# Sigmoid attention and a gated feed-forward layer on one core: other places for block sums on VectorE, and one copy on ScalarE

## The chip, the core and the metric

The kernel runs on one core of a Trainium2 chip. A core has five engines that run side by side, each through its own list of instructions and strictly in order: TensorE (PE in the profile; its weight loads are shown apart as PEld), VectorE (DVE), ScalarE (ACT), GpSimd (POOL) and SyncE (SP). Transfers run on 16 DMA engines, fed by queues: here POOL issues the input loads (queue q0), SP issues stores and DMA transposes (queue q1). The metric is the device time of one execution in microseconds (us), as a median of several.

## The reference

Inputs are q, k, v of shape 8 x 12 x 448 x 64 (batch, head, position, head dimension) and three weight matrices. What is computed:

```python
scores = scale * np.matmul(q, k.transpose(0, 1, 3, 2)) - np.log(S)
attn = 1.0 / (1.0 + np.exp(-scores))
attn_out = np.matmul(attn, v)
x = attn_out.transpose(0, 2, 1, 3).reshape(B * S, H * D)      # 3584 x 768
gate = np.maximum(x @ w_gate, 0.0)                            # 3584 x 1536
val = x @ w_val
out = gate * val @ w_out                                      # 3584 x 768
```

The attention is a sigmoid for each score, so it needs no sums over rows.

## The kernel before

**Tiling.** The data is held in fp16. Batches are handled one after another, 0 to 7. In a batch the 12 heads form three groups `g` of four heads, and the 448 keys form seven chunks `c` of 64. A *qk unit* (`qk_unit`, L292) is one chunk of one group: four matmuls into two PSUM banks, and ScalarE's sigmoid of each bank (L187) into a tile `PT`. After all seven chunks of a group, `pv_group` multiplies with v into two banks (28 matmuls), and VectorE scales those into `xT` (L184), the input of the feed-forward layer.

**Feed-forward, plain.** For batches 0 and 1 the layer is computed in the usual way. `gv` (L304) makes 128 of the 1536 hidden units: six matmuls with `wg` into `g_ps`, six with `wv` into `v_ps`, a ReLU of `g_ps` on ScalarE (`gate_sb`, L318) and the product on VectorE, which writes `hT` (L327) and so sets `v_ps` free. These pieces stand in `gv_queue`, and `ffn_mix` takes the next few of them; it also calls *hooks*, pairs of a number and a job, once no more than that number of pieces is left.

**Feed-forward, with block sums.** All else of the layer uses a Strassen-like scheme with seven block products where the usual one has eight. It needs sums and differences of blocks, all made on VectorE (`sub`, L376):
- `weight_sums(i)`, i = 0 to 3: four sums `T[i]` of blocks of `wo`, each 128 x 2304. `T[1]` is made from `T[0]`, and `T[3]` from `T[1]`.
- `token_sums` (L406): sums `S` of blocks of `hT` for one pair of token tiles.
- `gate_sums(f0, f1)` (L477): overwrites the upper half of `wv` by `wg - wv` for hidden tiles f0 and f0 + 1, 128 x 768 at once, six calls in all. This can only be done once the plain `gv` pieces that read those columns of `wv` are through; the plain pieces come in rising order of f.
- `unit_sums` and `batch_sums` for the block products of batches 2 and later.

`down_pair` (L423) makes the output of one pair of token tiles in seven products of six matmuls each, named by their PSUM tiles: b (`u`) = A11 B11; copy of b by `first_copy`; then `beside()`, which runs the jobs handed to it; c (`y12`) = S1 T[0]; b += S2 T[1]; a (`y11`) = A12 B21; b += S3 T[2]; c += S4 B22; b += A22 T[3]. Each accumulation into b must come after the earlier content of b was read out. The read-outs go to `ysb`: scaled copies on VectorE (`scaled`, L416) or ScalarE (`scaled_act`, L421), and multiply-and-add on VectorE (`plus`, L437).

**Transposes.** From batch 2 on, k and q get into the layout of TensorE through `dma_transposes` (L211): VectorE copies k and q of one group into `rel` (L215, two copies), and SP issues a DMA transpose of it into `qkT` (L219), which the qk units read.

**PSUM.** Eight banks are handed out in a ring (`bank`, L76): a tile gets the bank that was handed out eight calls ago (`down_pair` and the block form of the gate and value reorder the ring by `later`). TensorE waits there until the reader of the earlier content is through.

**Order.** The order of instructions is written out by hand: what the Python code emits first stands first in each engine's list. A batch is cut into stages m (`cuts`, L693 to L698). In a stage the qk units are emitted, with a `pv_group` between them, and then a piece of feed-forward work: pieces from `gv_queue` (the number is `mix[m]`), or one item of the list `work` by `next_work` (L675). For group 0 (batches 0 and 1) `work` holds ("y", 0, 0), ("t", 0, 6), ("y", 0, 1) and ("y", 0, 2): three `down_pair`s and one plain tile by `down` (L341).

What matters around the change:
- Batch 2, stage 4 takes one piece of `gv_queue`, stage 5 two, and then the first `down_pair` with the job `dma_transposes(3, 0), dma_transposes(3, 1)`. The four weight sums are hooks in these stages. `wo` is loaded by POOL behind batch 2's v and ahead of batch 3's k, q and v.
- Batch 3 takes one plain piece in each of stages 0, 1 and 2, the plain tile in stage 3, and the second `down_pair` in stage 4. All six `gate_sums` stand behind stage 3.

Of the kernel before, what the change touches and what calls it, by code (L numbers as in the profile page):

```python
# [17 lines left out]
def kernel(  # L18
# [19 lines left out]
    NFC = DF // P  # L38
# [37 lines left out]
    def bank(name, shape=(P, 512), dtype=FP32):  # L76
        pool, tag = free[0]
        free.rotate(-1)
        return pool.tile(list(shape), dtype, tag=tag, name=name)
# [4 lines left out]
    def later(order):  # L84
        keys = [free[i - 8] for i in order]
        for key in keys:
            free.remove(key)
            free.append(key)
# [286 lines left out]
    def sub(o, a, b):  # L375
        nc.vector.tensor_tensor(out=o, in0=a, in1=b, op=AOP.subtract)  # L376
# [5 lines left out]
    def products(jobs):  # L382
        for ps, n, kn, A, W, first in jobs:
            for k_ in range(kn):
                nc.tensor.matmul(  # L385
                    ps[:, 0:n],
                    A[:, k_, :],
                    W[:, k_, :],
                    start=(first and k_ == 0),
                    stop=(k_ == kn - 1),  # L390
                    skip_group_check=True,
                )


    def weight_sums(i):
        T = [late["T"][:, j] for j in range(4)]
        B11, B21 = wo[:, 0:HF, 0:HM], wo[:, HF:NFC, 0:HM]
        B12, B22 = wo[:, 0:HF, HM:DM], wo[:, HF:NFC, HM:DM]
        sub(T[i], *((B12, B11), (B22, T[0]), (B22, B12), (B21, T[1]))[i])

    def token_blocks(g, p):
        h = hT_tiles[g]
        t1, t2 = (slice(t * P, (t + 1) * P) for t in (2 * p, 2 * p + 1))
        return h[:, 0:HF, t1], h[:, HF:NFC, t1], h[:, 0:HF, t2], h[:, HF:NFC, t2]
# [15 lines left out]
    def scaled_act(o, ps):  # L420
        nc.scalar.activation(o, ps[:, 0:HM], AF.Copy, scale=OUT_SCALE)  # L421

    def down_pair(g, p, beside, then, last, first_copy):  # L423
        A11, A12, S3, A22 = token_blocks(g, p)
        S1, S2, S4 = sums.pop(("y", g, p))
        T1, T2, T3, T4 = (late["T"][:, i] for i in range(4))
        B11, B21, B22 = wo[:, 0:HF, 0:HM], wo[:, HF:NFC, 0:HM], wo[:, HF:NFC, HM:DM]
        y1, y2 = (ysbp.tile([P, DM], FP32, tag="ysb", name="ysb") for _ in range(2))
        lo, hi = slice(0, HM), slice(HM, DM)
        b, c, a = bank("u"), bank("y12"), bank("y11")  # L430
        later((7, 6, 5))

        def product(ps, A, W, first=True):
            products([(ps, HM, HF, A, W, first)])

        def plus(o, ps):
            nc.vector.scalar_tensor_tensor(  # L437
                out=o, in0=ps[:, 0:HM], scalar=OUT_SCALE, in1=o, op0=AOP.mult, op1=AOP.add
            )

        product(b, A11, B11)
        first_copy(y1[:, lo], b)
        beside()
        product(c, S1, T1)
        scaled_act(y2[:, hi], c)
        product(b, S2, T2, False)
        scaled_act(y1[:, hi], b)
        product(a, A12, B21)
        plus(y1[:, lo], a)
        if last:  # L450
            store(g, 2 * p, y1, 0, HM, (nc.sync, nc.sync))
        product(b, S3, T3, False)
        plus(y2[:, hi], b)
        if last:
            store(g, 2 * p + 1, y2, HM, DM, (nc.sync, nc.sync))
        product(c, S4, B22, False)
        plus(y1[:, hi], c)
        if last:
            store(g, 2 * p, y1, HM, DM, (nc.sync, nc.scalar))
        else:  # L460
            store(g, 2 * p, y1, 0, DM, (nc.sync, nc.sync))
        then()
        product(b, A22, T4, False)
        if last:
            q3 = slice(0, HM // 2), slice(HM // 2, HM)
            nc.scalar.activation(y2[:, q3[0]], b[:, q3[0]], AF.Copy, scale=OUT_SCALE)
            nc.vector.tensor_scalar(
                out=y2[:, q3[1]], in0=b[:, q3[1]], scalar1=OUT_SCALE, scalar2=None, op0=AOP.mult
            )
            store(g, 2 * p + 1, y2, 0, HM, (nc.sync, nc.scalar))  # L470
        else:
            scaled_act(y2[:, lo], b)
            store(g, 2 * p + 1, y2, 0, DM, (nc.sync, nc.sync))
# [185 lines left out]
    work = deque()  # L659
# [12 lines left out]
            elif kind == "y":  # L672
                token_sums(g, i)

    def next_work(jobs=(), alone=False):  # L675
        kind, g, i = work.popleft()

        def beside():
            for job in jobs:
                job()  # L680

        if kind == "y":
            down_pair(g, i, beside, prepare, not work, scaled_act if alone else scaled)
        elif kind == "w":
            gv_pair(g, i, lambda: (prepare(), beside()), nc.scalar.copy if alone else nc.vector.tensor_copy)
        else:
            beside()
            prepare()
            down(g, i)

    ffn_mix(1, [(1, lambda: both(1, 0))])
    for b in range(1, B):
        if b == 1:  # L693
            cuts, pv_at = (0, 3, 6, 9, 13, 17, 21), {3: (0, 2), 5: (1, 2)}
        elif b == 2:
            cuts, pv_at = (0, 4, 7, 11, 14, 18, 21), {0: (-1, 2), 2: (0, 2), 4: (1, 2)}
        else:
            cuts, pv_at = (0, 4, 8, 12, 16, 21), {0: (-1, 2), 2: (0, 2), 4: (1, 2)}  # L698
        count = len(cuts) - 1
        hooks = {}  # L700
        if b == 1:
            mix = (3, 3, 3, 3, 3, 2)
            hooks = {
                1: [(1, lambda: both(1, 1))],
                3: [(1, lambda: both(1, 2))],
                4: [(3, lambda: dma_transposes(2, 0))],
                5: [(2, late_loads)],
            }
        elif b == 2:
            mix = (2, 2, 1, 1, 1, 2)  # L710
            hooks = {
                2: [(0, prepare)],
                4: [(1, lambda: weight_sums(0)), (0, lambda: weight_sums(1))],
                5: [(1, lambda: weight_sums(2)), (0, lambda: weight_sums(3))],
            }
            open_late()
        elif b == 3:
            mix = (1, 1, 1, 0, 0)
        else:
            mix = (0,) * count  # L720
        for m in range(count):
            jobs = []
            for i, (g, c) in enumerate(order[cuts[m] : cuts[m + 1]]):
                if m in pv_at and i == pv_at[m][1]:
                    if m == 0:
                        pv_finish(b - 1)
                        if b == 2:
                            push_group(0)
                        elif b % 2 == 0:
                            push_group(b // 2 - 1)  # L730
                    else:
                        pv_group(b, pv_at[m][0])
                qk_unit(b, g, c)
            if m == 0 and b > 1:
                jobs.append(lambda: dma_transposes(b, 2))
            if b == 2 and m == count - 1:
                jobs.append(lambda: (dma_transposes(3, 0), dma_transposes(3, 1)))
            elif b == 3 and m == count - 1:
                jobs.append(lambda: (dma_transposes(4, 0), dma_transposes(4, 1)))
            elif 0 <= m - count + 2 and 3 < b < B - 1:  # L740
                jobs.append(lambda: dma_transposes(b + 1, m - count + 2))
            if b == 1:
                if m == 0:
                    load(2, 0, 1, "kq")
                    load(2, 1, 2, "kq")
                    load(2, 2, 3, "kq")
            elif m == 0 and b + 1 < B:
                if b == 3:
                    jobs.append(lambda: hold(3, 2))
                jobs.append(lambda: (load(b + 1, 0, 3, "kq"), load_v(b + 1)))  # L750
            if b % 2 and b > 2:
                if m == count - 1:
                    jobs.append(lambda: (batch_sums_t1(b // 2), batch_sums(b // 2, (0, 1))))
            elif b > 3 and m == 0:
                jobs.append(lambda: batch_sums(b // 2 - 1, (1, HD)))
            if b == 2 and m == count - 1:
                ffn_mix(mix[m], hooks[m])
                next_work(jobs)
            elif mix[m]:
                for job in jobs:  # L760
                    job()
                ffn_mix(mix[m], hooks.get(m, ()))
            else:
                next_work(jobs)
            if b == 3 and m == 3:
                for f in range(0, NFC, 2):
                    gate_sums(f, f + 2)
    pv_finish(B - 1)
    push_group(B // 2 - 1)
# [33 lines left out]
```

## Time and profile before

| | us |
|---|---|
| median of 3 runs | 400.2 (400.01 to 400.21) |
| the profiled execution | 400.3 |
| its span, first to last instruction | 398.5 |
| PE busy | 388.5 (97%) |
| DVE busy | 280.2 (70%) |
| ACT busy | 222.9 (56%) |
| POOL busy | 49.5 (12%) |
| granted TensorE clock, mean | 0.998 |

How to read the profile. Times are counted from the span's start. A line of the timeline gives the start, the length from the first start to the last end, the engine, the line in the kernel, the operation, what it writes and reads, and how many instructions were merged; in brackets stands how long the engine was idle before it and what ended that idle time. Matmuls are pipelined: one group's first matmul starts before the group before it has quite ended, so distances are best taken from start to start. A line of waits names the waiting engine, line and tile, what it waited for, the total, the number of waits and the longest. A line of windows gives the stretch, its length, the busy time of each engine (with the number of instructions), the granted TensorE clock, the mean share of the 16 DMA engines that was busy (it passes 1 where packets overlap) and GB/s. A line of a DMA queue gives packets, MB, and the packets' time as a share of 16 engines. Busy time off the engine that bounds a stage costs nothing there.

The two stretches that the change touches lie at 84 to 101 us (batch 2's last two stages) and at 107 to 130 us (batch 3's stages 1 to 4).

### The profile page before, as it was taken

The numbers are of one execution on the slowest core, as the hardware profiler recorded it, in microseconds if no ns is written. First come the engines' busy times: TensorE is split into PE (matmuls) and PEld (weight loads), VectorE is DVE, ScalarE is ACT, GpSimd is POOL, SyncE is SP. The second block draws the span as 40 slices with busy tenths as digits, with TensorE's granted clock in tenths as the row PEclk, the third lists the DMA queues.
The fourth block names the chain that finished last, engine by engine and source line by source line (L and its number), as shares of the span: only waits on it lengthen the run. The fifth ranks groups of instructions, "written<-read, shape, count | busy, mean of one in ns | idle before, by whom it ended". The sixth has DMA issues, their size and how long they took to land.

```text
span 398.5 us, 8744 instructions
## 1 busy us (share of the span) xinstructions
PE 388.5 (97%) x3488; PEld 217.6 (55%) x3488; DVE 280.2 (70%) x540; ACT 222.9 (56%) x475; POOL 49.5 (12%) x73
## 2 busy tenths in 40 slices
PE   8999999998998999999999999999999999999995
PEld 3678786444455555545555555455455555555563
DVE  2453344357358889999767889999775779987662
ACT  5946778783785465655675455565566233543121
POOL 9643301600030300003000210000000000000000
PEclk9999999999999999999999999999999999999999
DMA  9999994999897894223945696222113320000135
GB/s 149 199 198 205 204 157 81 178 203 178 187 152 152 169 208 79 46 48 43 169 90 133 134 207 109 47 16 55 27 33 88 81 79 2 0 1 2 39 92 147
DMA packets 68953, 43.69 MB, mean 110 GB/s; under 512 B 35888, under 2 KB 65584, under 8 KB 68912
## 3 DMA queue, kind: packets, MB, share of 16 engines
q0 software_dynamic: 30736, 23.33, 39.2%
q1 hardware_dynamic: 37744, 19.34, 23.0%
q8 instruction: 27, 0.44, 0.4%
q10 hardware_dynamic: 432, 0.46, 0.4%
q14 instruction: 14, 0.11, 0.1%
HBM read 47.19 MB, written 11.01 MB: 146 GB/s over the span
## 4 chain that ended last, share of the span: by engine, by line
PE 84%; DMA 10%; POOL 2%; DVE 2%; ACT 1%; issue 1%; ACTq 0%; POOLq 0%; DVEq 0%
PE u L385 32%; PE g L385 15%; PE y L385 9%; PE qk_ps L232 7%; PE pv_ps L250 7%; DMA wg<-in_moe_w_gate_dram 6%; PE g_ps L309 5%; PE v_ps L309 5%; DMA v<-in_v_dram 4%; PE ya L346 3%; PE yb L346 1%; POOL q L110 1%; ACT PT L187 1%; DVE wv L376 1%; POOL k L110 1%
## 5 line engine op out<-in xcount | busy, mean ns | idle before, releaser
L187 ACT ACTIVATE PT<-qk_ps 128x448 f16<-128x448 f32 (+3 forms) x318 | 150.6, 592 | 70.8 <-PE qk_ps L232 70.8
L385 PEld LDWEIGHTS <-S 128*128 128x128 f16 x540 | 52.8, 98 | 44.3 <-issue 0.8
L536 DVE TENSOR_TENSOR gsb<-g,gsb 128x448 f32<-128x448 f32 x72 | 43.0, 625 | 14.6 <-PE g L385 13.8
L232 PE MATMUL qk_ps<-qkT 64*64 64x448 f16 (+2 forms) x756 | 49.7, 336 | 0.8 <-DVE qkT L206 0.5
L421 ACT ACTIVATE ysb<-u 128x384 f32<-128x384 f32 x26 | 13.0, 498 | 52.5 <-PE u L385 52.5
L327 DVE TENSOR_TENSOR hT<-gate_sb,v_ps 128x256 f16<-128x256 f32 (+2 forms) x36 | 16.2, 465 | 33.0 <-ACT gate_sb L318 22.1
L385 PEld LDWEIGHTS <-hT 128*128 128x128 f16 x288 | 27.7, 98 | 21.0 <-issue 3.2
L532 ACT COPY gsb<-u 128x448 f32<-128x448 f32 x48 | 25.7, 564 | 23.9 <-PE u L385 22.9
L250 PE MATMUL pv_ps<-PT,v 64*64 64x448 f16 (+2 forms) x756 | 37.6, 329 | 0.7 <-DMA v<-in_v_dram 0.3
L184 DVE TENSOR_SCALAR xT<-pv_ps 128x448 f16<-128x448 f32 (+2 forms) x53 | 27.9, 566 | 13.8 <-PE pv_ps L250 12.4
L309 PE MATMUL v_ps<-xT,wv 128*128 128x256 f16 (+2 forms) x216 | 33.3, 290 | 0.7 <-DVE hT L327 0.7
L232 PEld LDWEIGHTS <-qkT 64*64 64x64 f16 x756 | 20.2, 105 | 24.9 <-issue 16.1
L309 PE MATMUL g_ps<-xT,wg 128*128 128x256 f16 (+2 forms) x216 | 33.5, 291 | 0.1
L385 PEld LDWEIGHTS <-wv 128*128 128x128 f16 x216 | 21.1, 98 | 19.7
L385 PEld LDWEIGHTS <-wg 128*128 128x128 f16 x216 | 20.3, 98 | 20.6 <-issue 3.0
L250 PEld LDWEIGHTS <-v 64*64 64x64 f16 x756 | 21.8, 107 | 12.4 <-issue 1.3
L385 PE MATMUL u<-T,hT 128*128 128x384 f16 x144 | 27.3, 326 | 0.0
L437 DVE SCALAR_TENSOR_TENSOR ysb<-y,ysb 128x384 f32<-128x384 f32 x24 | 13.4, 557 | 18.8 <-PE y L385 11.3
L110 POOL DMA_DIRECT2D k<-in_k_dram x14 | 10.9, 779 | 113.9 <-DVE rel L215 105.7
L309 PEld LDWEIGHTS <-wg 128*128 128x128 f16 x216 | 18.5, 98 | 11.5 <-issue 5.0
L309 PEld LDWEIGHTS <-wv 128*128 128x128 f16 x216 | 20.1, 98 | 8.3 <-issue 0.9
L385 PE MATMUL u<-xT,wg 128*128 128x448 f16 x108 | 23.5, 353 | 0.1
(69 smaller groups left out, 530.6 us busy)
## 6 DMA issues: line engine op xcount, KB each, us to landing
out_dram<-ysb SPq DMA_DIRECT2D x52, 192.0 KB, 3.0
k<-in_k_dram POOLq DMA_DIRECT2D x5, 672.0 KB, 12.1
q<-in_q_dram POOLq DMA_DIRECT2D x5, 672.0 KB, 14.7
v<-in_v_dram POOLq DMA_DIRECT2D x8, 336.0 KB, 15.5
v<-in_v_dram POOLq DMA_DIRECT2D x16, 168.0 KB, 15.6
k<-in_k_dram POOLq DMA_DIRECT2D x8, 224.0 KB, 10.4
wo<-in_moe_w_out_dram POOLq DMA_DIRECT2D x1, 1536.0 KB, 13.5
q<-in_q_dram POOLq DMA_DIRECT2D x6, 224.0 KB, 11.3
```

What stands on the lines that cost most here:

```text
L110: nc.gpsimd.dma_start(t16[:, xs, cs], rows_of(src, b)[:, xs, cs])
L184: nc.vector.tensor_scalar(out=xT, in0=src, scalar1=XSCALE, scalar2=None, op0=AOP.mult)
L187: nc.scalar.activation(PT_ap, ps_ap, AF.Sigmoid, bias=sig_bias, scale=qk_scale)
L232: nc.tensor.matmul(out_of(hh)[o : o + 64, :], qkT[rows, c, cols], qkT[rows, NCH + c0 : NCH + c1, cols], start=True, stop=True, tile_positi ...
L250: nc.tensor.matmul(ps[hh][64 * r : 64 * r + 64, 0:qn], v16[rows, 2 * g + hh, c * D : (c + 1) * D], pieces[c][rows, hh, :], start=(c == 0), ...
L309: nc.tensor.matmul(ps[-1][:, 0:qn], wt[:, dc, f * P : (f + 1) * P], xT_tiles[b][:, dc, q0 : q0 + qn], start=(dc == 0), stop=(dc == NDC - 1),)
L327: nc.vector.tensor_tensor(out=hT_tiles[g][:, f, o : o + qn], in0=gate_sb[:, 0:qn], in1=ps[1][:, 0:qn], op=AOP.mult,)
L346: nc.tensor.matmul(ps[:, 0 : m1 - m0], hT_tiles[g][:, f, t * P : (t + 1) * P], wo[:, f, m0:m1], start=(f == 0), stop=(f == NFC - 1),)
L385: nc.tensor.matmul(ps[:, 0:n], A[:, k_, :], W[:, k_, :], start=(first and k_ == 0), stop=(k_ == kn - 1), skip_group_check=True,)
L437: nc.vector.scalar_tensor_tensor(out=o, in0=ps[:, 0:HM], scalar=OUT_SCALE, in1=o, op0=AOP.mult, op1=AOP.add)
L532: by(gs[u][i][:], ps[u][:, 0:S])
L536: nc.vector.tensor_tensor(out=gs[u][i][:], in0=ps[u][:, 0:S], in1=gs[u][i][:], op=AOP.add)
```

## The change

Three things move, and no computation changes.

1. The hooks with the four weight sums. In batch 2's stage 4, sums 0 and 1 stood before and behind its one plain piece; now sum 0 stands behind it. In stage 5, sums 2 and 3 stood between its two pieces and behind them; now sums 1 and 2 stand there. Sum 3 becomes a further job of the first `down_pair`, behind the four `rel` copies of the two transposes.
2. In this first `down_pair` the copy of the first product is made by ScalarE instead of VectorE.
3. Of the six `gate_sums` calls of batch 3, the four for hidden tiles 0 to 7 now stand behind stage 1, and two stay behind stage 3.

On VectorE, the list between batch 2's stage 4 and the first `down_pair`'s last accumulations was: sum 0, hT, sum 1, hT, sum 2, hT, sum 3, first copy, four rel copies, three accumulations. It becomes: hT, sum 0, hT, sum 1, hT, sum 2, four rel copies, sum 3, three accumulations. On ScalarE one copy is added. The lists of TensorE, POOL and SP hold the same instructions in the same order.

```diff
-    def next_work(jobs=(), alone=False):
+    def next_work(jobs=(), alone=False, first_act=False):
...
-            down_pair(g, i, beside, prepare, not work, scaled_act if alone else scaled)
+            down_pair(g, i, beside, prepare, not work, scaled_act if alone or first_act else scaled)
...
-                4: [(1, lambda: weight_sums(0)), (0, lambda: weight_sums(1))],
-                5: [(1, lambda: weight_sums(2)), (0, lambda: weight_sums(3))],
+                4: [(0, lambda: weight_sums(0))],
+                5: [(1, lambda: weight_sums(1)), (0, lambda: weight_sums(2))],
...
-                next_work(jobs)
+                next_work(jobs + [lambda: weight_sums(3)], first_act=True)
...
-            if b == 3 and m == 3:
-                for f in range(0, NFC, 2):
+            if b == 3 and m in (1, 3):
+                for f in range(*((0, 8, 2), (8, NFC, 2))[m // 2]):
                     gate_sums(f, f + 2)
```

## The prediction

> **What bounds the kernel now.** I read the page's shares and chain, then who waited for whom with PE as the one that waits, then the timeline around those waits, then the DMA queues there.
>
> ```profile
> PE 388.5 (97%) x3488; PEld 217.6 (55%) x3488; DVE 280.2 (70%) x540; ACT 222.9 (56%) x475; POOL 49.5 (12%) x73
> PE 84%; DMA 10%; POOL 2%; DVE 2%; ACT 1%; issue 1%; ACTq 0%; POOLq 0%; DVEq 0%
> ```
>
> TensorE is busy for 97% of the span. The change touches no matmul, so it can gain only what PE waits for, and can lose only by making PE wait. The waits of PE:
>
> ```profile
> PE u L385 <- DVE xT L184: 1.2, 1, 1.2
> PE v_ps L309 <- DVE hT L327: 0.7, 1, 0.7
> PE u L385 <- DVE ysb L416: 0.6, 1, 0.6
> ```
>
> Three single waits, 2.5 us of idle, all for DVE. Two lie together (batch 2's end):
>
> ```profile
> 87.65 0.76 PE L232 MATMUL qk_ps<-qkT 64*64 64x448 f16 x12
> 88.34 1.31 PE L309 MATMUL g_ps<-xT,wg 128*128 128x448 f16 x6
> 88.38 1.36 DVE L376 TENSOR_TENSOR T<-wo 128x2304 f16<-128x2304 f16 x1 [2.22 <-DMA wo<-in_moe_w_out_dram]
> 89.65 0.61 DVE L327 TENSOR_TENSOR hT<-gate_sb,v_ps 128x448 f16<-128x448 f32 x1
> ...
> 90.32 1.30 PE L309 MATMUL v_ps<-xT,wv 128*128 128x448 f16 x6 [0.67 <-DVE hT L327]
> ...
> 94.53 1.35 DVE L376 TENSOR_TENSOR T<-wo,T 128x2304 f16<-128x2304 f16 x1
> ...
> 95.80 0.55 DVE L416 TENSOR_SCALAR ysb<-u 128x384 f32<-128x384 f32 x1
> 96.27 0.38 DVE L215 COPY rel<-k 128x896 f16<-128x896 f16 x1
> 96.40 1.14 PE L385 MATMUL u<-T,S 128*128 128x384 f16 x6 [0.57 <-DVE ysb L416]
> ```
>
> The first weight sum stands on DVE in front of a hidden-layer product and waits 2.22 us for `wo`; the product behind it frees the PSUM bank that v_ps wants. Later the fourth sum holds up DVE's copy of the first product. The third wait:
>
> ```profile
> 119.85 1.49 PE L250 MATMUL pv_ps<-PT,v 64*64 64x448 f16 x28
> 119.90 2.89 DVE L376 TENSOR_TENSOR wv<-wg,wv 128x768 f16<-128x768 f16 x6
> ...
> 122.71 1.15 DVE L184 TENSOR_SCALAR xT<-pv_ps 128x448 f16<-128x448 f32 x2
> 123.38 1.14 PE L385 MATMUL u<-wo,hT 128*128 128x384 f16 x6 [1.16 <-DVE xT L184]
> ```
>
> Six sums on `wv` stand ahead of the xT scaling; u takes pv's bank.
>
> **Change 1: the weight sums and the ScalarE copy.** With the hidden product ahead of the first sum, hT runs at about 87.8 (v_ps ends at 87.72; the usual lag is 0.10). The g group starts every 1.14 us or so, so v_ps starts at 89.48, not 90.32: **0.83**. The first sum still starts at 88.38, set by `wo`. DVE then has hT at 91.37 (behind ScalarE's gate at 90.70 + 0.60), the second sum at 91.9, hT at 93.2, the third at 93.74, the four rel copies from 95.01 (start to start, a sum takes 1.27, a copy 0.30, an hT 0.54), and the fourth sum at 96.21 to 97.56. PE: u at 92.89, then every 0.975: y 93.87, u 94.85, y 95.82, u 96.80, y 97.77, u 98.75. The last needs the fourth sum: 1.2 us to spare. The third product needs ScalarE's copy: u ends 94.03, the copy takes 0.49 (row of L421), free at 94.6, 0.2 to spare; ScalarE has nothing else then (it idles 2.54 us before its copy at 95.87). That takes away the second wait, 96.40 - 95.67 = **0.73**. The DVE accumulation into `y2`, which the last u needs, is behind the fourth sum and one other: 98.04 to 98.6, before 98.75. The last u moves from 100.30 to 98.75: 1.55 earlier.
>
> But what is late next? The qk of batch 3 behind this pair (PE 101.37 = 100.30 + 1.07, the same 1.07 as at 130.29 and 212.30, so nothing holds it up now) needs the DMA transpose of rel, issued on SP at 97.02, to land 4.1 us after (101.12), 0.25 ahead of its use. The rel copies are only 1.26 earlier, so SP issues at 95.76; q's load, which copy two reads, lands at 95.0 (73.7 + 21.3), just in time. At 4.1 us it would land at 99.86 and qk start near 100.0: a gain of 1.37. However, q0 is then still bringing in batch 3's v (landing 98.4 = 75.9 + 22.5):
>
> ```profile
> 97.00:97.50 0.50, 0.50 (x5) 0.29 (x3) 0.50 (x2) 0.00 (x0) 0.00 (x0) 1.00 0.17 23
> 98.25:98.50 0.25, 0.25 (x3) 0.14 (x2) 0.00 (x0) 0.00 (x0) 0.00 (x0) 1.00 1.00 201
> ...
> q0 software_dynamic: 27, 0.02, 17.2%
> ...
> q0 software_dynamic: 166, 0.15, 90.3%
> q1 hardware_dynamic: 170, 0.04, 32.9%
> ...
> q1 hardware_dynamic: 837, 0.21, 113.8%
> ```
>
> The first two lines are windows (last columns: DMA share, GB/s). From 96.8 to 98.1 the share is 0.17 against 1.26 with all 16 engines at work, so two engines lag with v packets (27 of them from 97 to 98); the transpose's own packets start at 98.2, 1.2 after its issue. From 140 to 141 a load and a transpose run together at one packet each (166 and 170); alone, q1 moves 837 in a microsecond (19 ns an engine). Moved up, the transpose starts at 96.95 and on two engines shares with about 16 v packets each, 69 ns apiece (231 per us over 16): 96.95 + 1.1 + 2.14 (448 KB at 837 packets per 0.21 MB, some 112 packets an engine) + 0.1 for alternating = 100.3, where it was 98.2 + 2.14 = 100.34. So it lands at about 101.0, hardly earlier than now, qk starts at 101.1 or 101.2, and PE idles some 1.3 us. I take **0.2** of the 1.55. Bounds: 1.55 if it lands within 3.9 (the shortest, at 164.1); -0.2 if it takes 5.7, the longest with a quiet q0 (217.4). I stay at 0.2 since the two engines' work is the same in either order.
>
> The Trainium skill, "DMA: Bandwidth & Descriptors", section "Queues, rings and completion order", says that each DMA engine alternates between the queue rows that have work, a packet of several descriptors at a time. It agrees with the 166 and 170 above and speaks against this move: by it the part is worth about 0.2, by the 4.1 us row alone 1.4.
>
> **Change 2: four of the six `wv` sums go to batch 3's second stage.** Two remain ahead of the xT scaling: 119.90 + 2 x 0.47 = 120.85, before pv is done. xT then starts 1.53 after pv's start as at 101.77/103.30: 121.38, freeing the bank at 122.0. PE also has three qk units to finish:
>
> ```profile
> 212.70 1.49 PE L250 MATMUL pv_ps<-PT,v 64*64 64x448 f16 x28
> 214.03 1.04 PE L232 MATMUL qk_ps<-qkT 64*64 64x448 f16 x12
> 215.00 0.28 PEld L385 LDWEIGHTS <-hT 128*128 128x128 f16 x3 [0.20 <-issue]
> ```
>
> Here the same sequence, without sums, has u 2.30 after pv's start. So u starts at 122.15, not 123.38: **1.23**. The bounds are 1.5 (12 qk matmuls in 0.69, as at 87.65) and 1.0 (a scaling 0.2 later). What follows u (first copy, rel copies, X sums, transposes, accumulations) hangs on u and moves with it; ScalarE's sigmoids now end 0.2 after y's product, which delays a copy nobody needs for four products.
>
> The four sums land behind hT at 110.50: 111.04 to 112.91. The xT pair behind them moves from 111.46 to 112.91 and frees its banks at 113.5 and 114.1; the ring of eight hands those to the first qk unit at 114.28. Cost nothing, margin 0.2; beyond it every delay is PE's, up to 0.5 if each sum stretches by 0.15. The next hT (114.46) waits for ScalarE's gate anyway. POOL issues batch 4's loads at 109.74 to 113.4 beside them; its issues took 0.87, 0.83, 0.75 and 1.26 also at 185.0 under a DVE 92 to 100% busy, so they stay. SP's and POOL's order is the same as before; the second and third transposes go out up to 1.4 earlier, and none is needed before 107.
>
> **Sum.** 0.2 + 1.23 = 1.4 us, in a PE-bound rest that only shifts. The profiled execution took 400.3 (span 398.5 and 1.8 around it), 0.1 above the median; from 400.2 I get **398.8**.
>
> **Rivals.**
> - *The transpose is not held up.* For it: 3.9 to 4.1 us in most rows. Against: the two lagging engines. Gain 1.37 + 1.23 = 2.6: 397.6. Chance 0.14.
> - *A transpose completes late.* At 62.7 and 217.4 with a quiet q0 it took 5.5 and 5.7, nothing else differing. If batch 3's first does so atop the sharing, or batch 4's first (0.4 to spare), 1.2 to 1.5 goes: 400.1. Chance 0.11.
> - *The sums in the second stage hold up xT.* Margin 0.2; 0.3 lost: 399.1. Chance 0.10.
> - *Slower: the transpose shares at full load.* If v's load ran on and all engines shared, it would take 10.6 to 12.4 us as at 226.5 and 135.0; issued at 95.76 it lands from 106.4, qk loses 5.1, sum 5.1 - 1.2: 404.1. It decides from a landing past 103.2. Against: q0 falls to 0.17 at 96.8, whatever the change. Chance 0.05.
>
> **How the numbers follow.** 398.8 has 0.60, its own range 398.4 to 399.2. The low end 397.4 takes in the free transpose with its 1.55 bound; the high end 399.9 reaches into the late completion. A measurement tells 0.2% (0.8 us) from nothing, so faster means below 399.4: 0.58 of the main case, all of the free transpose, 0.09 of the xT case: 0.81. Same: 0.02 + 0.01 and 0.09 of the late completion: 0.12. Slower: 0.07.
>
> **What would show it.** Right: neither v_ps near 89.5 nor the third product near 94.8 waits for DVE; last u at 98.7; PE's one new wait is qk for the transpose, 1 to 1.5 us, ending near 101.1; the transpose issued at 95.8 lands 5.2 after; u at 122 or so without a wait. Wrong: a landing 4.1 after the issue, a wait of qk for xT at 114, or a later last u.

## The result, and the profile after

The changed kernel takes 398.21 us (median of six runs, 397.81 to 399.14) against 400.11 for the kernel before: a ratio of 0.9953, 95% interval 0.9941 to 0.9964. It is faster by 1.9 us (1.4 to 2.4), where 1.4 was forecast. In two later comparisons the ratio was 0.9959 (0.9946 to 0.9972) and 0.9949 (0.9936 to 0.9963).

The execution that was profiled is the slowest of the six (399.14, span 397.3). It lost 1.0 us before the change is reached: the gate group of batch 2's stage 4 starts at 86.30 where it started at 85.28, and TensorE had waited for batch 1's v at 47 to 49 us. So positions are compared as distances from one start to another. Two stretches serve throughout:
- *stretch 1*, from the gate group of batch 2's stage 4 to the first qk unit of batch 3: 15.06 us (86.30 to 101.36) after 16.09 (85.28 to 101.37) before;
- *stretch 2*, from the first qk unit of batch 3's stage 4 to the second pair's first product: 2.70 (119.44 to 122.14) after 3.93 (119.45 to 123.38).

Together 2.26 us, and what follows only shifts: from that first product to the end of the span it is 275.2 now and 275.1 before.

Who waited for whom, TensorE as the one that waits, changed kernel:

```profile
PE pv_ps L250 <- DMA v<-in_v_dram: 0.8, 2, 0.5
PE qk_ps L232 <- DVE qkT L206: 0.5, 1, 0.5
PE qk_ps L232 <- DMA qkT<-rel: 0.4, 1, 0.4
```

The three waits for VectorE that the prediction showed are gone, and there is one new one: qk for the DMA transpose. The timeline of the changed kernel, batch 2's end and then batch 3's stages 1 to 4:

```profile
89.37 1.31 PE L309 MATMUL g_ps<-xT,wg 128*128 128x448 f16 x6
89.39 1.35 DVE L376 TENSOR_TENSOR T<-wo 128x2304 f16<-128x2304 f16 x1
...
90.52 1.30 PE L309 MATMUL v_ps<-xT,wv 128*128 128x448 f16 x6
...
96.00 0.39 DVE L215 COPY rel<-k 128x896 f16<-128x896 f16 x1
...
96.75 4.87 SPq L219 DMA_TRANSPOSE qkT<-rel  x2
...
97.21 1.35 DVE L376 TENSOR_TENSOR T<-wo,T 128x2304 f16<-128x2304 f16 x1
...
99.77 1.14 PE L385 MATMUL u<-T,hT 128*128 128x384 f16 x6
...
101.36 0.57 PE L232 MATMUL qk_ps<-qkT 64*64 64x448 f16 x8 [0.45 <-DMA qkT<-rel]
...
111.03 1.96 DVE L376 TENSOR_TENSOR wv<-wg,wv 128x768 f16<-128x768 f16 x4
...
112.91 1.15 DVE L184 TENSOR_SCALAR xT<-pv_ps 128x448 f16<-128x448 f32 x2
...
114.27 1.23 PE L232 MATMUL qk_ps<-qkT 64*64 64x448 f16 x16
...
121.37 1.16 DVE L184 TENSOR_SCALAR xT<-pv_ps 128x448 f16<-128x448 f32 x2 [0.47 <-PE pv_ps L250]
...
122.14 1.15 PE L385 MATMUL u<-wo,hT 128*128 128x384 f16 x6
```

What to see: v_ps now starts 1.15 behind its gate group, without a wait. The pair's last product stands 13.47 behind the first gate group (86.30 to 99.77), as worked out (98.75 - 85.28); the fourth sum, at 97.21, is done in time for it. Then qk comes 1.59 later instead of 1.07: the transpose was issued at 96.75 and landed 4.6 after. At 114.27 the delayed xT scalings cost nothing, and at 122.14 the second pair starts at the place that was forecast (122.15).

### The profile page after: what moved, and what is told of

Read it like the earlier page. It is cut to its first block, busy times and chain, and to the rows that moved or that the text cites. A ratio compares the mean times of both kernels' runs of the same rounds, so it can differ in the third digit from the quotient of the medians.

```text
span 397.3 us, 8744 instructions
## 1 busy us (share of the span) xinstructions
PE 388.5 (98%) x3488; PEld 217.5 (55%) x3488; DVE 279.6 (70%) x539; ACT 223.2 (56%) x476; POOL 49.5 (12%) x73
## 4 chain that ended last, share of the span: by engine, by line
PE 84%; DMA 11%; POOL 2%; ACT 1%; issue 0%; DVE 0%; ACTq 0%; POOLq 0%; DVEq 0%
PE u L385 32%; PE g L385 15%; PE y L385 8%; PE qk_ps L232 7%; PE pv_ps L250 7%; PE g_ps L309 5%; PE v_ps L309 5%; DMA wg<-in_moe_w_gate_dram 4%; DMA v<-in_v_dram 3%; PE ya L346 3%; DMA q<-in_q_dram 2%; PE yb L346 1%; DMA qkT<-rel 1%; ACT PT L187 1%; POOL k L110 1%; POOL q L110 1%
```

## The experiments

Two readings of the new wait were held against each other. *Shared engines*: the transpose is late because the last packets of batch 3's v still occupy DMA engines. *Own time*: a transpose takes 4.1 to 4.6 us after its issue whatever runs beside it, and the prediction saw sharing where there was none. Stretch 1 and the landing tell them apart; the times tell whether a stretch reaches the end.

### The changed kernel again, and each half alone

The first run is the changed kernel as it is.

> The changed kernel once more, as the measure for the three others. Both theories: about 1.9 us less than the kernel before (398.2 against 400.1). From the start of the gate group of batch 2's stage 4 to the first qk of batch 3: 15.1 us (16.09 before, 15.06 in the first profile of the changed kernel). From that first qk unit of batch 3's stage 4 to the first product of the second pair: 2.70 us (3.93 before).

Measured: 398.36 us, ratio 0.9959 (0.9946 to 0.9972), so 1.64 us; stretch 1 15.10, stretch 2 2.70. Then only the `wv` sums:

```diff
-            if b == 3 and m == 3:
-                for f in range(0, NFC, 2):
+            if b == 3 and m in (1, 3):
+                for f in range(*((0, 8, 2), (8, NFC, 2))[m // 2]):
```

> Only the four wv sums are moved. Both theories: 1.23 us less than before, so 398.9. The stretch to batch 3's first qk stays at 16.1 us, the one to the second pair's first product is 2.70 us.

Measured: 398.84 us, ratio 0.9969 (0.9958 to 0.9979), so 1.24 us with 0.84 to 1.68 as the interval; stretch 2 is 2.70. Stretch 1 was expected to stay at 16.1 and was 15.73. Its first wait was smaller in this execution; timeline:

```profile
87.82 1.36 DVE L376 TENSOR_TENSOR T<-wo 128x2304 f16<-128x2304 f16 x1 [1.85 <-DMA wo<-in_moe_w_out_dram]
...
88.16 1.31 PE L309 MATMUL g_ps<-xT,wg 128*128 128x448 f16 x6
...
89.10 0.61 DVE L327 TENSOR_TENSOR hT<-gate_sb,v_ps 128x448 f16<-128x448 f32 x1
...
89.77 1.29 PE L309 MATMUL v_ps<-xT,wv 128*128 128x448 f16 x6 [0.30 <-DVE hT L327]
```

VectorE waited 1.85 us for `wo` instead of 2.22, and TensorE 0.30 instead of 0.67, with the same code in this stretch. The wait that the other half of the change removes is as long as the load of `wo` happens to be late against TensorE, and that differed between these two executions.

The other half alone, the weight sums and the ScalarE copy:

```diff
-            if b == 3 and m in (1, 3):
-                for f in range(*((0, 8, 2), (8, NFC, 2))[m // 2]):
+            if b == 3 and m == 3:
+                for f in range(0, NFC, 2):
```

(against the changed kernel)

> Only the weight sums and the ScalarE copy. By the working of the prediction 0.2 us less than before (399.9), the stretch to batch 3's first qk 15.9. By the profile of the changed kernel 1.0 less (399.1), the stretch 15.1. The second stretch stays at 3.93.

Measured: 399.49 us, ratio 0.9982 (0.9973 to 0.9991), so 0.72 us with 0.36 to 1.08 as the interval; stretch 1 15.01, stretch 2 3.92. The prediction's 0.2 is outside. The halves give 1.24 + 0.72 = 1.96 together; the whole gave 1.64 in this same comparison, with 1.1 to 2.2 as the interval, and 1.9 in the first. They add up within the noise.

### Take the load away from the transpose, and add to it

```diff
-                jobs.append(lambda: (load(b + 1, 0, 3, "kq"), load_v(b + 1)))
+                jobs.append(lambda: (load(b + 1, 0, 3, "kq"), b > 2 and load_v(b + 1)))
...
-                jobs.append(lambda: (dma_transposes(3, 0), dma_transposes(3, 1)))
+                jobs.append(lambda: (dma_transposes(3, 0), dma_transposes(3, 1), hold(3, 0), load_v(3)))
```

> The changed kernel, with batch 3's v loaded only after the first transpose of batch 3 has landed, so that no load runs beside that transpose. Theory of the shared engines: the transpose lands 4.0 to 4.1 us after its issue, qk waits 0.1 or not at all, the stretch is 14.6 to 14.7 and the time 0.4 below the changed kernel's. Theory that the landing takes its own time, whatever q0 carries: 4.6 after the issue again, stretch 15.1, time as the changed kernel's.

Measured: the transpose landed 4.1 after its issue, qk did not wait, and stretch 1 was 14.56. The floor is 14.54, the 16.09 of before less the 1.55 that the last product gains. So the load beside the transpose sets the delay, and *own time* is out. Whether the two share the engines or something else on their way, this run cannot tell. But the time was 399.93, ratio 0.9992: slower than the changed kernel. TensorE's timeline of this run says where it went:

```profile
109.44 0.35 PE L250 MATMUL pv_ps<-PT,v 64*64 64x448 f16 x2
110.25 0.37 PE L250 MATMUL pv_ps<-PT,v 64*64 64x448 f16 x1 [0.46 <-DMA v<-in_v_dram]
111.39 1.51 PE L250 MATMUL pv_ps<-PT,v 64*64 64x448 f16 x25 [0.77 <-DMA v<-in_v_dram]
```

The first value product of batch 3 now waits for v, with some 1.8 us from start to start beyond its usual course (109.44 to 112.56 and not 1.36). That was the run's own price, which its expectation had left out.

The opposite: more load beside the transpose.

```diff
-                jobs.append(lambda: (load(b + 1, 0, 3, "kq"), load_v(b + 1)))
+                jobs.append(lambda: (load(b + 1, 0, 3, "kq"), load_v(b + 1), b == 2 and nc.gpsimd.dma_start(
+                    late["X"][:, 0:2].rearrange("p a k s -> p (a k) s"), rows_of(v, 3)
+                )))
```

> The changed kernel with batch 3's v read once more into a scratch tile right behind the load of v, so that q0 is busy on all engines some 3.4 us longer. Shared engines: the transpose, issued at the same place, gets one packet for one of the load's, lands 7 to 8 us after its issue instead of 4.6, and the stretch grows to about 17.5 to 18.5. Own time: 4.6 and 15.1.

Measured (one run): landing 7.8 after the issue, stretch 1 18.32 (85.55 to 103.87). That is within what was expected of shared engines and far from the own time. The time was 404.27, some 6 us above the changed kernel's, and the wait explains only 3.3 of it; the rest is in the section on the hardware.

### A version that keeps the transpose free

Since only a third of v is needed early, the load can be cut: the third for group 0 where it was, the rest behind the first transpose's landing.

```diff
-                jobs.append(lambda: (load(b + 1, 0, 3, "kq"), load_v(b + 1)))
+                jobs.append(lambda: (load(b + 1, 0, 3, "kq"), load_v(b + 1, 0, 2 if b == 2 else NPAIR)))
...
-                jobs.append(lambda: (dma_transposes(3, 0), dma_transposes(3, 1)))
+                jobs.append(lambda: (dma_transposes(3, 0), dma_transposes(3, 1), hold(3, 0), load_v(3, 2)))
```

(`load_v(b, x0, x1)` loads head pairs x0 to x1.)

> The changed kernel, with batch 3's v loaded in two steps: its first third, which the first value product of batch 3 needs, where it was, and the other two thirds once the first transpose of batch 3 has landed. Shared engines: the first third is in about 2.2 us sooner than all of v was, so most of the sharing goes; the transpose lands 4.1 to 4.3 after its issue, the stretch from the gate group of batch 2's stage 4 to batch 3's first qk is 14.6 to 14.8 instead of 15.06 to 15.10, no value product waits for v, and the time is 0.3 to 0.5 below the changed kernel's (397.9). Own time: 4.6 and 15.1 again, 398.3.

Measured: landing 4.1 after the issue, stretch 1 14.57, no value product of batch 3 waits; 398.0 us, ratio 0.9942 (0.9926 to 0.9958). Run once more on one chip with the changed kernel:

> The changed kernel, beside the next two on one chip: stretch 15.1, 0.4 to 0.5% below the kernel before.

> The kernel with batch 3's v in two steps again, now beside the changed kernel: stretch 14.57 as in its first profile, 0.5 us below the changed kernel if a shorter stretch reaches the end; the same time if it is given back later.

Measured: 398.19 us (0.9949, 0.9936 to 0.9963) for the changed kernel with stretch 1 14.94, and 397.82 (0.9943, 0.9930 to 0.9955) for this one with 14.66. In every profile its stretch is the shorter one, by 0.3 to 0.5, and its median is 0.4 lower; but the intervals overlap, so the time does not prove the gain over the changed kernel. Against the kernel before it is clear.

The windows of the first transpose show the three cases side by side. The stretch, its length, busy time by engine, and at the end the granted clock, the DMA share and GB/s. Before:

```profile
98.50:99.00 0.50, 0.50 (x6) 0.29 (x3) 0.45 (x1) 0.00 (x0) 0.00 (x0) 1.00 1.12 215
99.00:99.50 0.50, 0.50 (x5) 0.30 (x4) 0.11 (x1) 0.00 (x0) 0.00 (x0) 1.00 1.16 214
```

Changed (its transpose's packets start at about 97.9, v's last leave at about 98.7):

```profile
98.50:99.00 0.50, 0.50 (x5) 0.31 (x4) 0.50 (x2) 0.00 (x0) 0.00 (x0) 1.00 1.01 60
99.00:99.50 0.50, 0.50 (x5) 0.30 (x4) 0.46 (x2) 0.00 (x0) 0.00 (x0) 1.00 0.88 114
...
100.00:100.50 0.50, 0.50 (x5) 0.31 (x4) 0.46 (x1) 0.00 (x0) 0.00 (x0) 1.00 1.28 286
```

With v cut in two:

```profile
97.50:98.00 0.50, 0.50 (x5) 0.30 (x4) 0.50 (x2) 0.00 (x0) 0.00 (x0) 1.00 1.12 216
98.00:98.50 0.50, 0.50 (x5) 0.31 (x4) 0.46 (x2) 0.00 (x0) 0.00 (x0) 1.00 1.16 212
```

In these windows the transpose alone moves 212 to 217 GB/s. In the changed kernel the rate falls to 60 GB/s around the end of v, and afterwards it reaches 286. The packets of the changed kernel, by half microseconds from 98.0 to 100.5 (q1 carries the transpose, q0 the load of v; a line of q1 alone is a half microsecond without v):

```profile
q1 hardware_dynamic: 368, 0.09, 155.1%
q0 software_dynamic: 16, 0.01, 16.8%
...
q1 hardware_dynamic: 96, 0.02, 93.4%
q0 software_dynamic: 8, 0.01, 7.2%
...
q1 hardware_dynamic: 223, 0.06, 87.8%
...
q1 hardware_dynamic: 462, 0.12, 128.3%
...
q1 hardware_dynamic: 559, 0.14, 127.8%
```

Alone, before the change, q1 moves 420 and 417 in the half microseconds from 98.5 to 99.5. So the transpose first runs near its rate beside v's last packets, then drops to 96. That is not just two engines' part: at the usual rate the other 14 would have moved some 370. Over the first three half microseconds it falls some 570 packets short, 0.7 us of its work; over the next two it gains some 185, or 0.2 us. The other six profiles with the same load there fall to between 28 and 120 GB/s in their lowest half microsecond. Why the end of a load holds up all of the transpose is not shown. The landing loses 0.3 to 0.5 (4.4 to 4.6 against 4.1), not the 1.1 of the prediction.

### Which of the moved sums matter

First the ScalarE copy undone:

```diff
-                next_work(jobs + [lambda: weight_sums(3)], first_act=True)
+                next_work(jobs + [lambda: weight_sums(3)])
```

> The changed kernel with the first product's copy back on VectorE. The third product of the first pair waits for the copy, which stands behind the third weight sum: 0.7 us. If the transpose sets what comes after, as in the changed kernel, only 0.2 to 0.3 of that is paid (the last product still ends before or close to the landing, and the rel copies are 0.47 later): stretch 15.3 to 15.4, time 0.2 to 0.4 above the changed kernel's. If PE's own chain set it, the whole 0.7: stretch 15.8.

Measured: the third product waits for the copy as before (at 96.30, idle 0.57 for VectorE), stretch 1 is 15.37, and qk follows the last product by 1.17, so product and landing end nearly together. 398.51 us, ratio 0.9954 (0.9939 to 0.9970); 0.3 us cannot be told in the time. The copy's 0.73 on TensorE is worth about 0.3, since the transpose takes the rest.

Then the weight sums 1 to 3 back where they were, with the copy on ScalarE kept:

```diff
-                4: [(0, lambda: weight_sums(0))],
-                5: [(1, lambda: weight_sums(1)), (0, lambda: weight_sums(2))],
+                4: [(0, lambda: (weight_sums(0), weight_sums(1)))],
+                5: [(1, lambda: weight_sums(2)), (0, lambda: weight_sums(3))],
...
-                next_work(jobs + [lambda: weight_sums(3)], first_act=True)
+                next_work(jobs, first_act=True)
```

> The changed kernel with the weight sums 1 to 3 in their old places: sum 0 and sum 1 behind the piece of stage 4, sums 2 and 3 in stage 5 as before, the ScalarE copy and the four wv sums as changed. If only the place of sum 0 and the ScalarE copy matter: the rel copies start at the same point (VectorE has the same number of sums ahead of them less one, and waits less), stretch 15.1, time as the changed kernel. If moving the fourth sum behind the rel copies matters: stretch longer by up to 1.27, one sum.

Measured: stretch 1 15.05, 398.36 us, ratio 0.9955 (0.9942 to 0.9967). The rel copies start 9.70 behind the gate group, as in the changed kernel (96.00 - 86.30 = 9.70). VectorE had idle time in front of the second hidden product, into which sum 1 fits. So of the first change only two edits work: sum 0 behind its piece, and the copy on ScalarE. Moving the fourth sum behind the rel copies bought nothing.

### The margin in batch 3's second stage

```diff
                     gate_sums(f, f + 2)
+                if m == 1:
+                    for f in (0, 2):
+                        fs = slice(f * P, (f + 2) * P)
+                        sub(late["X"][:, 1, :, 0 : 2 * P], wg[:, 0:HD, fs], wv[:, 0:HD, fs])
```

> The changed kernel with two more sums of 128 x 768 behind the four wv sums of batch 3's stage 1, into a scratch tile: work added, nothing taken out. If the margin of the xT scalings was 0.2 us as worked out from the ring of banks: the first qk unit of stage 3 waits for xT on VectorE, 0.2 and then up to 0.5 more for the second bank, and the time is 0.5 to 0.8 above the changed kernel's. If VectorE's work in this stage costs nothing: no wait and no change. The second pair's first product is still 2.70 after the stage's first qk.

Measured, from TensorE's timeline of this run:

```profile
114.09 0.35 PE L232 MATMUL qk_ps<-qkT 64*64 64x448 f16 x1 [0.29 <-DVE xT L184]
114.62 0.95 PE L232 MATMUL qk_ps<-qkT 64*64 64x448 f16 x15 [0.19 <-DVE xT L184]
```

The first matmul waits for the first bank and the second for the other, as the ring of banks said. From stage 2's gate group to stage 4's first qk it is 8.33 (111.35 to 119.68) instead of 7.55, so 0.78 later; 399.10 us, ratio 0.9973, about 0.6 to 1.0 us above what the changed kernel's ratios give. The xT scalings start 1.05 later (2.07 behind the gate group, 113.42 - 111.35, instead of 1.02, 112.91 - 111.89), so some 0.27 of that was free, where a margin of 0.2 had been worked out. Six sums in this stage cost time; four fit.

## Why the prediction was right, and where it was off

- **What bounds it.** Right: the three waits for VectorE are gone, and the two stretches that held them are where the time was gained.
- **Change 2, 1.23 us.** Right to the hundredth in stretch 2 (3.93 to 2.70 in every profile with the moved sums). In the time it was 1.24, with 0.84 to 1.68 as the interval, so that closeness is luck. The row that carried it was the same sequence later in the kernel, where u stood 2.30 behind pv.
- **Four sums in the second stage cost nothing, margin 0.2.** Right: no wait with four, waits with six, and a margin of some 0.27. The rival that put 0.3 there did not come.
- **The order on VectorE and TensorE, last u 1.55 earlier.** Right: 13.47 in both.
- **What is late next.** The kind was right: the transpose takes back part of the 1.55, as one new wait of qk, because the end of v's load lies beside it. *The step that failed is the term "I take 0.2 of the 1.55"*: stretch 1 got 1.03 shorter in the first profile, and the half alone brought 0.72 us (0.36 to 1.08). The landing was put at 5.2 after the issue and came at 4.6 (4.4 to 4.6 in all seven profiles with the same load beside it). The working took 19 ns a packet, read where all 16 engines ran transposes together, as the speed of one lagging engine by itself, and added v's packets in front of it. The runs show instead that the transpose hardly slows while v's last packets leave, falls 0.7 us of its work short around their end, on more than the two engines that lag, and regains 0.2. Without a load beside it the landing is 4.1 and the stretch 14.57: the overlap costs 0.4 to 0.5 of the stretch, not 1.1. Why the transpose slows in this way stays open.
- **A wait taken from one execution.** The 0.83 of the first wait was 0.47 in another execution of the same code there (from the starts at 88.16 and 89.77, less 1.14). The profile's 16.09 is thus the larger of the two values seen with the old code (the other is 15.73), which may be one reason why the time gained (1.9) is less than the 2.26 of the two profiles.
- **The rival of the free transpose** (397.6) did not happen, but the cut load makes it real: 14.57, and 397.8 to 398.0 us. **The slower rival** (a transpose at full load) was made to happen by the extra load: landing 7.8 after the issue, 404.27 us. It was priced at 404.1 from a later landing, without the fall of the clock, so the close figures are a coincidence. **The late completion** was not seen at batch 3's first transpose.
- The Trainium skill, "DMA: Bandwidth & Descriptors", section "Queues, rings and completion order", has each DMA engine alternate between the queue rows that have work, a packet at a time. The extra load's 7.8 and the free 4.1 agree with that; for the short overlap the estimate from alternation gave 5.2, and 4.4 to 4.6 was measured.

## What to carry to other kernels

When a stall goes, work out what is late next from its own queue, and look at what else that queue's engines carry at the new, earlier time; here the tail of a load, which had left just before the transpose's first packets, came to lie upon them. Look in the profile for another place where the same sequence runs without the suspected stall: its spacing gives the new time directly. And a wait that a load sets can differ by tenths of a microsecond from execution to execution (0.67 and 0.30 here), so its gain is a range even where the order of instructions is certain.

## What the runs showed of the hardware

With the extra load TensorE stood idle for 3.7 us, and its granted clock fell to one half and stayed there for some 7 us. Windows of that run (granted clock is the third number from the end):

```profile
99.00:101.00 2.00, 1.15 (x8) 0.49 (x5) 0.56 (x1) 0.49 (x1) 0.00 (x0) 1.00 1.26 205
101.00:103.00 2.00, 0.00 (x0) 0.00 (x0) 0.00 (x0) 0.00 (x0) 0.00 (x0) 0.91 1.30 169
103.00:104.00 1.00, 0.13 (x4) 0.14 (x8) 0.00 (x0) 0.00 (x0) 0.00 (x0) 0.50 1.28 256
104.00:106.00 2.00, 2.00 (x24) 0.98 (x24) 0.00 (x0) 1.45 (x4) 0.00 (x0) 0.50 1.12 239
106.00:108.00 2.00, 2.00 (x24) 0.74 (x16) 0.53 (x1) 0.49 (x2) 0.00 (x0) 0.50 0.77 264
108.00:109.00 1.00, 1.00 (x7) 0.44 (x4) 1.00 (x4) 1.00 (x3) 0.00 (x0) 0.50 0.00 0
109.00:110.00 1.00, 1.00 (x6) 0.45 (x4) 0.23 (x1) 0.77 (x2) 0.00 (x0) 0.78 0.00 0
110.00:112.00 2.00, 2.00 (x23) 0.78 (x21) 0.62 (x1) 0.93 (x2) 0.00 (x0) 1.00 0.84 159
```

The value product behind the wait took 2.61 us from its start to the next group's (104.61 to 107.22) instead of 1.32 (101.76 to 103.08 in the changed kernel). The wait of 0.45 in the changed kernel and the 1.16 of the kernel before leave the clock at 1.00. In this one run the wait thus cost 3.3 us in stretch 1 and 2.7 more behind it: from that first qk to the one of batch 3's second stage it is 7.26 (103.87 to 111.13) instead of 4.58 (101.36 to 105.94).
